# Retention and a squared-ReLU feed-forward on one core: the first four chunks stay in two-token rows through the attention

## The chip, the cores and the metric

The kernel runs on one core of a Trainium2 chip. The metric is device time in microseconds (us), as the median of several runs. One further execution is profiled; every row, wait and chain quoted in this document comes from such a profiled execution, and "the span" is its length from the first to the last recorded event.

The core has five engines with a queue each. TensorE (PE) multiplies matrices and also transposes, VectorE (DVE) and ScalarE (ACT) do elementwise work and are the ones that read TensorE's output memory PSUM, GpSimd (POOL) does elementwise work on SBUF alone, and SyncE (SP) issues the transfers (DMA) here.

## The reference

Two stages. The first is a retention layer: per batch (4) and head (8) a 64x64 state runs over 768 tokens, decays by a factor gamma of its head at each token and takes in the outer product of k and v; the output is q times the state, scaled. The second is a feed-forward on the 3072x512 result.

```python
for t in range(S):
    state = gamma[None, :, None, None] * state + np.einsum('bhd,bhe->bhde', k[:, :, t], v[:, :, t])
    y[:, :, t] = scale * np.einsum('bhd,bhde->bhe', q[:, :, t], state)
...
h = np.maximum(x @ w_in, 0.0)
return (h * h @ w_out).astype(np.float32)
```

Here x is y laid out as tokens by 512 features, w_in is 512x2048 and w_out is 2048x512. Inputs and output are float32; the kernel computes in bf16 with float32 accumulation.

## The kernel before

**Tiles.** The 3072 tokens are 24 chunks of 128 (six per batch). The recurrence is done in blocks: inside a state step the contribution of tokens is q times k, masked, times v; what came earlier is q times the state. Decay is put into tables, so that v is multiplied by `vf` (a growing factor per token) when it is cast, and the result by `yf` (a falling one) when it leaves PSUM. A state step covers 64 tokens, so a chunk has two. Per chunk the attention issues, on TensorE, `scores` (line 576, q times k into the PSUM tile `sc`), `sums` (line 587, k times v for the state, also into `sc`), `values` (line 550, masked scores times v into `yy`) and `apply` (line 565, q times state into `yy`). A `visit` is one such round; DVE then masks the scores (`P`, line 630), updates the state twice (`S`, lines 641 and 643), and multiplies the output into the feed-forward's input tile `xt` (`Y`, line 652). All matmuls of a visit are 64x64x64, spread over the four quadrants of the array.

**The first four chunks** come in two pairs (`together`, two calls, chunks 0 and 1, then 2 and 3). A pair's q, k and v are loaded so that a partition holds two neighbouring tokens (512 bytes in a piece in place of 256), one 512 KB transfer for each of q, k, v. They are cast into `twin` tiles (which live in the third hidden tile `h2`, shown as `h` in the profile). Then q and k are transposed on TensorE (`T`, line 434) and copied out (`E`), and k and v are put into normal token order by matmuls with a 0/1 matrix `perm` (`N`, line 459), each with a copy out of PSUM (`M`). After that the ordinary visits follow. Later chunks are loaded one by one; their q and k are transposed on TensorE (line 533) for chunks 4 to 7 and by a DMA after that.

**Feed-forward.** `ffn1` multiplies `xt` with `w_in` (line 699) block by block; a block is 1, 2 or 4 chunks (`BLOCKS`), and a group of matmuls always fills one PSUM bank (16 matmuls of 128 columns, 8 of 256 or 4 of 512). ACT applies ReLU (line 704), DVE squares (line 709). `ffn2` multiplies with `w_out` (line 743), four matmuls of 512 columns per quarter of w_out, ACT copies out (line 751) and SP stores.

**Weights** are loaded as float32 in pieces (`w_in` as four half quarters of 512 KB and two quarters of 1 MB, `w_out` as four quarters of 1 MB) through four staging tiles `wst` and cast in parts by DVE, ACT or POOL.

**Order.** Nothing is ordered by hand except the transfers, whose order is the string `ORDER` (`q0` is the q load of the first pair, `i0` the first piece of w_in, `o0` of w_out). Everything else is added to a `Plan` with an engine or several to choose from, assumed durations, the tiles it reads and writes, and a priority; `schedule` places the operations one after another, the earliest start first, and the program is emitted in that order, so that each engine's queue is fixed in advance. The plan also inserts filler matmuls on the identity (line 794), and `PRE` = 20 matmuls of one element at the very start (line 790). `SPLIT` says how many visits are split into two halves, `NPE` and `NTD` where the transposes change their kind (chunks from NPE to NTD are transposed by small flips inside a visit).

Of the kernel before, what the change touches and what calls it, by code (L numbers as in the profile page):

```python
# [15 lines left out]
ALU = mybir.AluOpType  # L16


class Plan:
# [21 lines left out]
    def add(self, name, eng, dur, reads=(), writes=(), fn=None, prio=0.0, lat=0.0, bank=None, after=(), count=0):  # L41
# [15 lines left out]
        if not isinstance(eng, dict):  # L57
            eng, flex = {eng: dur}, False
        else:
            flex = True  # L60
        self.ops.append(dict(i=i, name=name, eng=eng, flex=flex, deps=sorted(deps), fn=fn,
# [136 lines left out]
BLOCKS = [2, 1, 1, 1, 1, 2, 2, 2, 4, 4, 4]  # L198
SPLIT = 6
AHEAD = 4  # L200
WARM = 16.0
FILL = 0.215
WARMING = 5.5
PACE = 6
LEAD = 2
NPE = 8
NTD = 8
PRE = 20
# [3 lines left out]
TCAST = {'ACT': 0.63, 'POOL': 0.78}  # L212
TEVAC = {'ACT': 0.6}
MEVAC = {'ACT': 0.6, 'DVE': 0.62}
# [8 lines left out]

ORDER = (
    "o0 k0 v0 o1 q0 v2 k2 o2 q2 o3 i0 i1 i2 i3 q4 i4 v4 i5 k4 k5 v5 q5 k6 v6 q6 q7 v7 k7"
# [11 lines left out]
def kernel(  # L237
# [38 lines left out]
    def sb(name, shape, dt):  # L276
# [16 lines left out]
    perm = sb("perm", [P, 2, P], BF16)  # L293
    ex2_i = sb("ex2_i", [P, NCH // 2, 2], I32)
    ex2_f = sb("ex2_f", [P, NCH // 2, 2, H], FP32)
    vf2 = sb("vf2", [P, NCH // 2, 2, H], FP32)
# [5 lines left out]
             for j in range(2)]  # L302
    pos_i = h2s[NH2 - 1][:, 12:15, :].rearrange("p a n -> p (a n)").bitcast(I32)
# [15 lines left out]
    def where(m):  # L319

        return divmod(m, NCH)
# [27 lines left out]
    def placing():  # L349

        nc.gpsimd.memset(perm[:], 0.0)
        for half in range(2):
            r = slice(L * half, L * half + L)
            nc.gpsimd.affine_select(out=perm[r], in_=perm[r], compare_op=ALU.not_equal,
                                    fill=1.0, base=0, pattern=[[-1, 2], [1, P]], channel_multiplier=-2)
# [7 lines left out]
    pl.add("perm", "POOL", 1.2, (), ("perm",), placing, prio=-95.5)  # L363
# [15 lines left out]
               out=ex2_f[:], in0=ex2_i[:, :, :, None].to_broadcast([P, NCH // 2, 2, H]),  # L379
               in1=lng[:, None, None, :].to_broadcast([P, NCH // 2, 2, H]), op=ALU.mult), prio=-99)  # L380
# [5 lines left out]
    def ytable():  # L386
        for p in range(NJ):
            nc.scalar.activation(yf[:, p, :], pos_i[:], AF.Exp, scale=lnt[:, p : p + 1])
    yf_made = pl.add("yf", "ACT", 3.4, ("pos_i", "lnt"), ("yf",), ytable, prio=-98)
# [10 lines left out]
    twin_users = [yf_made]  # L400

    def together(n):
# [3 lines left out]
        m, s0, w, twin = 2 * n, (2 * n) % NLD, n % 2, twins[n % 2]  # L406
# [8 lines left out]
        for g in range(2):  # L415
            for x in "kq":
                o = twin[x][:, g, :].rearrange("s (j a d) -> s a j d", a=2, j=NJ)
                t = rows_(x).rearrange("s (a j g d) -> s a j g d", a=2, j=NJ, g=2)[:, :, :, g, :]
                pl.add(f"c{x}{m}.{g}", TCAST, 0, held(x), (f"twin{x}{w}.{g}",),
                       lambda on, t=t, o=o: copy_on(on, o, t), prio=urgency(m))  # L420
            t = rows_("v").rearrange("s (h g d) -> s h g d", h=H, g=2)[:, :, g, :]
            pl.add(f"cv{m}.{g}", CVT, 0, held("v") + ("vf2",), (f"twinv{w}.{g}",),
                   lambda on, t=t, g=g: (nc.vector if on == "DVE" else nc.gpsimd).tensor_tensor(  # L423
                       out=twin["v"][:, g, :].rearrange("s (h d) -> s h d", h=H), in0=t,
                       in1=vf2[:, i // 2, g, :, None].to_broadcast([P, H, D]), op=ALU.mult),
                   prio=urgency(m))
        q0 = m % NQT
        for x, name in enumerate("kq"):
            o1 = {}

            def turn_fn(g, x=x, name=name, o1=o1):
                ps = fps[o1["op"]["bank_index"]].bitcast(BF16)
                for j in range(NJ):
                    nc.tensor.transpose(ps[:, 512 * g + j * P : 512 * g + j * P + P],  # L434
                                        twin[name][:, g, j * P : j * P + P], ident[:])
            for g in range(2):
                i0 = pl.add(f"T{name}{m}.{g}", "PE", 0.26, (f"twin{name}{w}.{g}", "ident"), (f"gT{name}{m}{g}",),
                            lambda g=g, turn_fn=turn_fn: turn_fn(g),
                            prio=-200 + m, lat=0.2, count=4, after=twin_users[-1:] if g else (),
                            bank=("open", ("T", m, x), False) if g == 0 else ("use", ("T", m, x)))  # L440
                twin_users.append(i0)
                if g == 0:
                    o1["op"] = pl.ops[i0]
            for c in range(2):
                pl.add(f"E{name}{m}.{c}", TEVAC, 0,
                       [f"gT{name}{m}{g}" for g in range(2)], [f"qkT{q0 + c}.{name}"],
                       lambda on, x=x, c=c, o1=o1: copy_on(
                           on, qkts[q0 + c][:, x].rearrange("p j (t g) -> p j t g", g=2),
                           fps[o1["op"]["bank_index"]].bitcast(BF16).rearrange("p (g j c t) -> p c j t g", g=2, j=NJ, c=2)[:, c]),
                       prio=urgency(m + c), lat=0.05, bank=("close", ("T", m, x), 2))  # L450
        for c in range(2):
            r = slice(L * c, L * c + L)
            for name in "kv":
                o1 = {}

                def place(name=name, r=r, o1=o1):
                    ps = fps[o1["op"]["bank_index"]]
                    for g in range(2):
                        nc.tensor.matmul(ps[:], lhsT=perm[r, g, :], rhs=twin[name][r, g, :], start=(g == 0), stop=(g == 1))  # L459
                i0 = pl.add(f"N{name}{m + c}", "PE", 0.45, (f"twin{name}{w}.0", f"twin{name}{w}.1", "perm"), (f"gN{name}{m + c}",),  # L460
                            place, prio=-190 + m + c, lat=0.2, count=2, bank=("open", ("N", m + c, name), False))
                twin_users.append(i0)
                o1["op"] = pl.ops[i0]
                o = bf[name][(m + c) % NBF]
                o = o.rearrange("s j a d -> s (j a d)") if name == "k" else o.rearrange("s h d -> s (h d)")
                pl.add(f"M{name}{m + c}", MEVAC, 0, (f"gN{name}{m + c}",), (f"bf{name}{(m + c) % NBF}",),
                       lambda on, o=o, o1=o1: copy_on(on, o, fps[o1["op"]["bank_index"]][:]),
                       prio=urgency(m + c), lat=0.05, bank=("close", ("N", m + c, name)))
# [122 lines left out]
    def visit(m, n, t=None):  # L591
# [55 lines left out]
        if m is not None:  # L647
# [3 lines left out]
            pl.add(f"Y{m}", "DVE", 0.68, ("yy0", "yy1", "yf"), (f"xt{g % NXT}.{u}",),  # L651
# [29 lines left out]
    def ffn1(blk):  # L681
# [5 lines left out]
        for f0 in range(0, NFB, per):  # L687
# [19 lines left out]
            def square(f0=f0):  # L707
# [10 lines left out]
                   after=twin_users if g == NH2 - 1 else ())  # L718
# [45 lines left out]
    for m in range(-1, NM):  # L764
# [5 lines left out]
        if n < SPLIT:  # L770
            if m >= 0:
                visit(m, None)
            visit(None, n, t)
        else:
            visit(m, n if n < NM else None, t)
# [52 lines left out]
```

## Time and profile before

| | us |
|---|---|
| median of 6 runs | 212.51 (212.14 to 212.95) |
| the profiled execution | 212.11 |
| its span | 210.3 |
| TensorE busy in the span | 198.4 (94%) |
| VectorE busy | 115.5 (55%) |
| ScalarE busy | 90.9 (43%) |
| GpSimd busy | 42.8 (20%) |
| first feed-forward matmul starts | 19.79 |
| last matmul ends | 207.11 |

TensorE's busy time is the union of matmuls whose ends are modelled, so 94% is a share of time with something in the array, not of its peak. Where a row of the timeline ends in brackets, they give the idle time before it and what ended it. "Issue" in a chain is time in which the engine waited for nothing that the profile shows. In a list of waits the engine and line that waited come first, then what was waited for, the total, the number of times and the longest.

### The profile page before, as it was taken

How to read it: one execution, taken by the hardware profiler on the slowest of the kernel's cores; microseconds unless marked ns; L12 is line 12 of the kernel's file. 1: busy time of each engine (PE TensorE's matmuls, PEld its weight loads, DVE VectorE, ACT ScalarE, POOL GpSimd, SP SyncE). 2: the span in 40 equal slices, each digit the busy share in tenths (PEclk: the TensorE clock that was granted, in tenths of full speed). 3: DMA queues.
4: the chain of work that ended last, by engine and by line, in shares of the span. 5: the costliest groups of instructions: out<-in, count | busy, mean ns of one | idle time of the engine just before them, and what ended most of it. 6: DMA issues, size and time to landing. Idle time of an engine off the chain costs nothing.

```text
span 210.3 us, 6166 instructions
## 1 busy us (share of the span) xinstructions
PE 198.4 (94%) x2683; PEld 117.8 (56%) x2683; DVE 115.5 (55%) x253; ACT 90.9 (43%) x154; POOL 42.8 (20%) x72
## 2 busy tenths in 40 slices
PE   1797899999999999999999999999999999999993
PEld 1354798676766858767644444444444444444452
DVE  2557977866565956676756573667554433322100
ACT  8575667552332524444222644323533324534221
POOL 6653313233322211312222031222000000000000
PEclk9999999999999999999999999999999999999999
DMA  6999999999999999999999999999211011011022
GB/s 160 290 315 324 348 354 344 342 188 251 218 191 248 196 209 221 212 169 243 208 204 176 191 248 166 238 211 227 49 53 53 0 65 38 0 50 51 0 103 100
DMA packets 94443, 38.15 MB, mean 181 GB/s; under 512 B 79952, under 2 KB 88400, under 8 KB 94416
## 3 DMA queue, kind: packets, MB, share of 16 engines
q1 hardware_dynamic: 94416, 37.76, 83.4%
q8 instruction: 21, 0.34, 0.7%
q14 instruction: 6, 0.05, 0.1%
HBM read 27.26 MB, written 6.29 MB: 160 GB/s over the span
## 4 chain that ended last, share of the span: by engine, by line
PE 92%; DMA 3%; issue 1%; SPq 1%; POOL 1%; ACT 0%
PE fps L743 40%; PE fps L699 40%; DMA vn<-in_v_dram 3%; PE yy L550 3%; PE yy L565 2%; PE sc L587 2%; PE sc L576 2%; SPq L411 1%; PE fps L459 1%; PE fps L533 1%; POOL h L423 1%; PE fps L434 1%; PE fps L794 0%; ACT osb L751 0%
## 5 line engine op out<-in xcount | busy, mean ns | idle before, releaser
L743 PE MATMUL fps<-w_out,h 128*128 128x512 bf16 (+1 forms) x400 | 92.4, 371 | 0.0
L699 PE MATMUL fps<-xt,w_in 128*128 128x128 bf16 (+2 forms) x704 | 92.4, 282 | 0.0
L704 ACT ACTIVATE h<-fps 128x512 bf16<-128x512 f32 x96 | 57.3, 597 | 71.3 <-PE fps L699 71.2
L699 PEld LDWEIGHTS <-w_in 128*128 128x128 bf16 x704 | 58.3, 98 | 28.7
L709 DVE TENSOR_TENSOR h<-h 128x512 bf16<-128x512 bf16 x96 | 42.7, 452 | 52.5 <-ACT h L704 52.2
L743 PEld LDWEIGHTS <-h 128*128 128x128 bf16 x400 | 37.3, 98 | 36.9
L751 ACT ACTIVATE osb<-fps 128x512 f32<-128x512 f32 (+1 forms) x25 | 14.5, 580 | 35.8 <-PE fps L743 35.8
L397 POOL CAST kqs<-kn 128x512 bf16<-128x512 f32 x20 | 13.3, 666 | 66.1 <-DMA kn<-in_k_dram 58.2
L652 DVE TENSOR_TENSOR xt<-yy,yf 128x512 bf16<-128x512 f32 x24 | 16.5, 686 | 13.8 <-PE yy L565 12.6
L643 DVE TENSOR_TENSOR state<-sc,state 128x256 bf16<-128x256 f32 x40 | 16.8, 419 | 0.7
L630 DVE TENSOR_TENSOR pt<-sc,cmask 128x512 bf16<-128x512 f32 x24 | 16.4, 682 | 1.4 <-PE sc L587 1.2
L491 DVE TENSOR_TENSOR vs<-vn,vf 128x512 bf16<-128x512 f32 x20 | 15.1, 757 | 2.1 <-DMA vn<-in_v_dram 1.9
L397 POOL CAST kqs<-qn 128x512 bf16<-128x512 f32 x20 | 13.0, 650 | 11.9 <-DMA qn<-in_q_dram 11.8
L565 PE MATMUL yy<-qkT,state 64*64 64x64 bf16 x352 | 11.9, 198 | 0.5
L550 PEld LDWEIGHTS <-vs 64*64 64x64 bf16 x384 | 5.1, 107 | 8.5 <-issue 8.1
L587 PE MATMUL sc<-vs,kqs 64*64 64x64 bf16 x352 | 7.8, 195 | 1.5 <-issue 1.5
L393 ACT ACTIVATE qkT<-fps 128x512 bf16<-128x512 bf16 x12 | 6.7, 596 | 5.2 <-PE fps L533 3.1
L550 PE MATMUL yy<-pt,vs 64*64 64x64 bf16 x384 | 7.8, 198 | 0.6 <-issue 0.6
L434 PE MATMUL fps<-ident,h 128*128 128x128 bf16 x32 | 3.8, 273 | 4.5 <-POOL h L397 4.5
L565 PEld LDWEIGHTS <-state 64*64 64x64 bf16 x352 | 7.3, 107 | 1.1 <-PE yy L565 1.1
L576 PE MATMUL sc<-qkT 64*64 64x64 bf16 x384 | 7.6, 196 | 0.0
L587 PEld LDWEIGHTS <-kqs 64*64 64x64 bf16 x352 | 5.6, 109 | 1.6 <-issue 1.6
(51 smaller groups left out, 69.6 us busy)
## 6 DMA issues: line engine op xcount, KB each, us to landing
out_dram<-osb SPq DMA_DIRECT2D x23, 256.0 KB, 4.0
qn<-in_q_dram SPq DMA_DIRECT2D x20, 256.0 KB, 5.3
vn<-in_v_dram SPq DMA_DIRECT2D x20, 256.0 KB, 4.7
kn<-in_k_dram SPq DMA_DIRECT2D x20, 256.0 KB, 5.3
wst<-in_moe_w_out_dram SPq DMA_DIRECT2D x4, 1024.0 KB, 10.0
wst<-in_moe_w_in_dram SPq DMA_DIRECT2D x4, 512.0 KB, 8.4
wst<-in_moe_w_in_dram SPq DMA_DIRECT2D x2, 1024.0 KB, 10.1
kn<-in_k_dram SPq DMA_DIRECT2D x2, 512.0 KB, 5.8
```

What stands on the lines that cost most here:

```text
L397: nc.gpsimd.tensor_copy(o, t)
L491: lambda: nc.vector.tensor_tensor(out=o[:], in0=t.rearrange("s (h d) -> s h d", h=H), in1=vf[:, i, :, None].to_broadcast([P, H, D]), op=AL ...
L550: nc.tensor.matmul(yy[L * c : L * c + L, sub, p * L : p * L + L], lhsT=vs[r, 4 * a + j, :], rhs=pt[r, a, j, :], start=(p == 0), stop=True, ...
L565: nc.tensor.matmul(yy[L * c : L * c + L, sub, p * L : p * L + L], lhsT=st[r, j, :], rhs=qkT[r, 1, j, sub * L : sub * L + L], start=False, ...
L587: nc.tensor.matmul(sc[L * a : L * a + L, sub, 256 + j * D : 256 + j * D + D], lhsT=ks[r, j, a, :], rhs=vs[r, 4 * a + j, :], start=False, s ...
L630: lambda: nc.vector.tensor_tensor(out=pt[:], in0=sc[:, :, 0:256].rearrange("s g (p t) -> s g p t", p=NJ), in1=cmask[:, None, None, :].to_b ...
L643: f = lambda cc=cc, j1=j1, j0=j0: nc.vector.tensor_tensor(out=sts[j1][:], in0=cc, in1=sts[j0][:], op=ALU.add)
L652: lambda: nc.vector.tensor_tensor(out=xt[:, :, u * C : u * C + C].rearrange("s p (g t) -> s g p t", g=2), in0=yy[:, :, 0:256].rearrange("s ...
L699: nc.tensor.matmul(ps[:, u * n : u * n + n], lhsT=w_in_bf[j][:, cb, c * P : (c + 1) * P], rhs=xt[:, cb, cols], start=(cb == 0), stop=(cb = ...
L704: nc.scalar.activation(h2[:, f0 : f0 + per, cols], ps[:].rearrange("p (u n) -> p u n", u=per), AF.Relu)
L709: nc.vector.tensor_mul(hv, hv, hv)
L743: nc.tensor.matmul(ps[:, 0:w], lhsT=h2[:, fb, u * C : u * C + C], rhs=w_out_bf[j][:, c, ns], start=(fb == 0), stop=(fb == NFB - 1))
```

## The change

The pairs are no longer put into normal token order. The eight `N` products with `perm` (two matmuls each) and the eight copies `M` go, and with them `perm`. Instead the attention of the first four chunks works on a pair as it lies, with g the place of a token in its two-token row (0 or 1) and c the half of the partitions (so c is the chunk): scores and masked scores are made per g (`pair_scores`, `P`), the state step is 128 tokens (one per chunk), and `pair_values` and `pair_sums` add the two places in PSUM. The matmuls of `pair_scores`, `pair_values` and `pair_apply` have 128 columns. The work is divided by halves of the heads (b2): `sc` serves one half, `yy` the other. So a pair has two `A` (scores, 16 matmuls each), four `P`, two `B` (sums, 16 each; the last chunk of a batch would need none), two `S`, two `C` (values and state, 20 to 24 matmuls with a drain and a wait between the two parts of the state) and two `Y`.

What else changes with it: the casts of a pair are divided by heads (`.0`, `.1`) and may also run on DVE; a half's transposes have a bank of their own and one copy out, four per pair, on ACT or DVE; masked scores of a pair (`pts2`) live in the second hidden tile, so that its ReLU waits for the pairs; `yf` is made in four separate operations; chunks 2 and 3 form one block of the feed-forward; there are no one-element matmuls at the start (`PRE` 0); chunk 7 is transposed by flips (`NPE` 7); the order of the transfers changes; and a few casts are bound to an engine (`HOME`).

The core of the diff:

```diff
+        if name in HOME:
+            eng = {HOME[name]: eng[HOME[name]]}
+        prio = RANK.get(name, prio)
...
-BLOCKS = [2, 1, 1, 1, 1, 2, 2, 2, 4, 4, 4]
+BLOCKS = [2, 2, 1, 1, 2, 2, 2, 4, 4, 4]
-WARM = 16.0
+WARM = 20.0
-PACE = 6
+PACE = 8
-NPE = 8
+NPE = 7
-PRE = 20
+PRE = 0
-TCAST = {'ACT': 0.63, 'POOL': 0.78}
-TEVAC = {'ACT': 0.6}
-MEVAC = {'ACT': 0.6, 'DVE': 0.62}
+TCAST = {'DVE': 0.43, 'ACT': 0.63, 'POOL': 0.78}
+TEVAC = {'ACT': 0.6, 'DVE': 0.62}
...
+HOME = {'ck5': 'ACT', 'cq5': 'ACT', 'Eq0.0': 'DVE', 'cv0.0': 'DVE', 'ck0.0': 'DVE', 'cwin5.2': 'DVE', 'cv2.1': 'POOL', 'ck2.0': 'DVE', 'cwin5.0': 'DVE', 'cwin2.0': 'POOL', 'cwout0.3': 'POOL', 'cwin1.0': 'POOL', 'ck0.1': 'DVE', 'ck2.1': 'DVE'}
 ORDER = (
-    "o0 k0 v0 o1 q0 v2 k2 o2 q2 o3 i0 i1 i2 i3 q4 i4 v4 i5 k4 k5 v5 q5 k6 v6 q6 q7 v7 k7"
+    "q0 k0 o0 i0 v0 q2 k2 o1 v2 i1 v4 i2 k4 i3 i4 q4 i5 k5 v5 v6 o2 o3 q5 v7 k6 q6 k7 q7"
 )
...
-    perm = sb("perm", [P, 2, P], BF16)
+    cmask2 = sb("cmask2", [P, 2, C], BF16)
+    pts2 = [h2s[1][:, 4 * j : 4 * j + 4, :].rearrange("p (b a) (g j t) -> p b a g j t", b=2, g=2, j=2) for j in range(2)]
...
-                        nc.tensor.matmul(ps[:], lhsT=perm[r, g, :], rhs=twin[name][r, g, :], start=(g == 0), stop=(g == 1))
...
+    def pair_scores(m, b2):
+        t = pair_qk(m)
+        for g in range(2):
+            for j in range(2):
+                for a in range(2):
+                    r = slice(L * a, L * a + L)
+                    for c in range(2):
+                        nc.tensor.matmul(held_by[b2][L * c : L * c + L, a, (2 * g + j) * C : (2 * g + j + 1) * C],
+                                         lhsT=t[r, 0, b2, c, j, L * g : L * g + L], rhs=t[r, 1, b2, c, j, :],
+                                         start=(g == 0 and j == 0), stop=True, skip_group_check=True)
...
+    def pair_sums(m, c, ps):
+        kt, vt = pair_tiles(m)
+        r = slice(L * c, L * c + L)
+        for g in range(2):
+            for j in range(NJ):
+                for a in range(2):
+                    nc.tensor.matmul(ps[L * a : L * a + L, j * D : j * D + D], lhsT=kt[r, j, a, g, :], rhs=vt[r, 4 * a + j, g, :],
+                                     start=(g == 0 and j == 0), stop=True, skip_group_check=True)
...
+            for a in range(2):
+                pl.add(f"P{m}.{b2}{a}", "DVE", 0.68, (banks[b2][a], "cmask2"), (f"ptp{w}.{b2}{a}",),
...
+            def values_and_state(b2=b2):
+                pair_values(m, b2)
+                pair_apply(m, b2, 0)
+                nc.tensor.drain(fusable=True).then_inc(turn, 1)
+                turns[0] += 1
+                nc.tensor.wait_ge(turn, turns[0])
+                pair_apply(m, b2, 1)
...
-                   after=twin_users if g == NH2 - 1 else ())
+                   after=twin_users if g == NH2 - 1 else pt_users if g == 1 else ())
...
-        if n < SPLIT:
-            if m >= 0:
+        if n < 2 * NPAIR:
+            if n % 2 == 0:
+                pair_visits(n)
+        elif n < SPLIT or m < 2 * NPAIR:
+            if m >= 2 * NPAIR:
```

## The prediction

> **What bounds the kernel now.** I read the page's engine shares first, then TensorE's list of waits, then the chain of waits at the start and around 44 us, then the timeline for when tiles of the inputs arrive.
>
> ```profile
> PE 198.4 (94%) x2683; PEld 117.8 (56%) x2683; DVE 115.5 (55%) x253; ACT 90.9 (43%) x154; POOL 42.8 (20%) x72
> ```
>
> ```profile
> PE fps L434 <- POOL h L397: 4.5, 1, 4.5
> PE sc L587 <- issue: 1.5, 1, 1.5
> PE fps L459 <- DVE kqs L395: 0.8, 1, 0.8
> ...
> PE yy L550 <- issue: 0.6, 1, 0.6
> ```
>
> TensorE bounds it. Its few waits are all early, and the list holds only what its queue waited for; so the question is how early it becomes full, and how much work it then has. The chain, start, length and what:
>
> ```profile
> 12.18 1.04 PE fps L459 x4
> ...
> 15.33 0.54 PE fps L459 x2
> ...
> 17.28 0.53 PE fps L459 x2
> ...
> 18.16 1.48 issue
> 19.64 0.22 PE sc L587 x4
> 19.86 1.85 PE fps L699 x16
> ...
> 25.77 0.61 issue
> ```
>
> ```profile
> 42.88 1.79 PE fps L699 x32
> 44.67 0.86 PE fps L743 x4
> ...
> 195.83 11.28 PE fps L743 x68
> 207.13 0.38 ACT osb L751
> ```
>
> The reordering matmuls (L459) stand three times on the chain, 2.1 us in all, the feed-forward begins at 19.79, and after the stop at 25.77 there is no further one: TensorE works through to 207.11, and a tail of 3.2 us (copy, store) closes the span of 210.3. The two "issue" stops come after 449 and 705 TensorE instructions of the program (weight loads and matmuls counted), 256 apart. The times at which inputs are there are read where a cast starts that waited for a DMA:
>
> ```profile
> 5.21 1.17 POOL L397 CAST h<-kn 128x512 bf16<-128x512 f32 x2 [0.84 <-DMA kn<-in_k_dram]
> 7.03 1.54 POOL L423 TENSOR_TENSOR h<-vn,vf 128x512 bf16<-128x512 f32 x1 [0.66 <-DMA vn<-in_v_dram]
> ...
> 15.65 0.61 POOL L397 CAST w_in<-wst 128x512 bf16<-128x512 f32 x1 [0.88 <-DMA wst<-in_moe_w_in_dram]
> ```
>
> Likewise 8.73, 10.53, 12.33, 14.15 for the other pair loads: one 512 KB pair load per 1.8 us. Half pieces of w_in come at 15.65, 17.16, 19.71, 21.32 (1.5 us each, later ones shared with a q load), and the last quarter of w_out at about 42.6.
>
> **What the skill says.** "Runtime: NRT & Kernel Launch", Instruction fetch mechanics: instructions are refilled in blocks of 256, at a cost "mostly hidden". The 256 between the two stops fits; hidden they are not here, 1.48 and 0.61 us. The DMA view shows one instruction packet between 17.0 and 17.5 and one between 23.6 and 24.1: TensorE passed its 193rd instruction at 14.1 and resumed past the 449th at 19.64 (5.5 us later), passed that and resumed past the 705th at 26.38 (6.7 us later). So while inputs stream, a block needs 5.5 to 6.7 us from the passing of the edge before. "TensorE: Matmul & The Clock Gate", Part 1: the clock is halved until about 3.4 us of sustained work. The trace agrees: two 256-column fillers take 0.61 us at 13.15 and 0.38 at 16.25. Same page, Part 3: matmuls in different quadrants run concurrently; the trace shows 16 scores of 64 columns in 0.13 us on the chain, four at a time. "VectorE: DVE Perf Modes", mode 2x_2P: PSUM has one read port, so no doubled rate from there; masking 128x512 out of PSUM takes 0.682 us here, a cast from SBUF 0.41.
>
> **The change part by part.** Removed: 16 matmuls `N` (2.1 us on the chain, the rest before 10) and eight copies `M` of 0.6 to 0.69 us, four each on DVE and ACT. Added on DVE: four more `P` (0.682 each) and five casts (0.41 to 0.43). The 20 one-element matmuls at the start (0.64 us at 0.77, while nothing else could run) cost nothing either way, except that the 40 instructions less move the block edges. Two costs are not shown: a matmul of 64x64x128, and an interleaving copy of q out of PSUM on DVE. The first lies between 16 in 0.13 us (bound by issue, no dearer than 64 columns) and 16 in 0.45 (two at a time at 56 ns each); I take four at a time (16 matmuls of 128 columns take 0.89 us in the feed-forward, 56 ns each), 0.23, at half clock 0.43. The second lies between 0.425 (plain bf16 copy, DVE row) and 0.69 (cast from PSUM); I take 0.65. Below nothing neither can be.
>
> I walk the new queues with these rows. Loads: q0 5.2, k0 6.95, w_in piece 0 8.45, v0 10.25, q2 12.05, k2 13.85, v2 15.65, w_in piece 1 17.15. q casts and transposes 5.2 to 6.7, k casts on DVE to 7.85, copies of q and k to 8.65 and 9.2, scores at half clock until 9.9. Then v0: its POOL half takes 1.54 and ends at 11.8; `B` from 11.87 to 12.95; DVE meanwhile does v 10.96, two masks 12.32, `S` twice until 13.42, last mask 14.1. `C` of half 0 starts at 13.47 (0.95 at half clock), `Y` ends 15.2; `C` of half 1 ends 15.65 and its `Y` 16.4. The second pair's scores half 0 go at 16.65, and **the feed-forward starts at 17.0** in place of 19.79: weights and `xt` are there.
>
> From there DVE sets the pace, with nothing idle: copy of k 16.85, masks 17.8 and 18.5, third mask 19.2, `S` 19.7 and 20.15 (behind `B` at 18.85, which waits for both v casts of 1.54 on POOL), last mask 20.85, one square 21.3, the v cast of chunk 4 22.0, `Y` 22.7 and 23.4. TensorE does three groups of the first block (0.875 each) in between and then stands until 23.45 for `xt` of chunks 2 and 3. From there it is full: 13 groups of 256 columns (11.4), 4 of 128 (3.6), 6 quarters of ffn2 (5.2), three transposes (0.65), one visit in halves and a half (1.1) make 21.9 and reach the first product with the last quarter of w_out at **45.4**. That quarter: three small loads more stand ahead of it than before (786 KB, 2.25 us at 350 GB/s), so it lands at 44.9 and is cast at about 45.8. I take **45.8**.
>
> What remains then, against the kernel before at 44.67, where it starts the same product: two groups of 128 columns (1.79), one ffn2 quarter (0.865) and half a visit (0.2) less, and transposes: five of 0.22 before, two plus a round of flips (0.26) now, 0.4 less. So 207.11 - 44.67 - 3.25 = 159.2, TensorE ends at 205.0, the span is 208.2. Every hop between engines in the early walk was put at 0.05 us; I allow 0.4 for what is late there. **Span 208.6**, execution 210.4; the profiled execution of before is 0.4 below its median, so the median becomes **210.8**.
>
> The instruction stops: edge 193 is passed in the first `C` at 13.8, so the block past 449 (in the third `C`, 20.3) is there at 19.3 to 20.5, hidden by the wait for DVE; the next edge, 705, is not reached before 31. Cover gone, 0.2 us. Waits added: `C` waits on `S` and mask, and behind it stand transposes of the next pair and a feed-forward group; they are counted above. ReLU of the second hidden tile now waits for both pairs, long done by then. Casts of w_in on POOL stand behind three v casts: piece 1 at 19.4 and piece 2 at 20.2 instead of landing plus 0.6; that delays the second group to 19.4, under DVE's chain.
>
> **Rivals.** (1) The clock is late: TensorE's early work is sparser than before (idle from 9.9 to 11.87, hardly any fillers), so full clock may come only 3.4 us after 17.0. Then the first group takes 1.71, the scores of half 1 of the second pair end at 19.4 in place of 18.3, every DVE step after moves by 0.9 and TensorE is full at 24.35: the product with the last quarter starts at 46.3 plus the same 0.4, so 211.3. For it: 17.0 to 20.4 is the first unbroken stretch; against: before, some 5 us of nearly unbroken work (8.8 to 14) were enough to raise it. (2) The weights are late: loads share 16 engines, and one v load took 9 us from issue to landing in the trace before. With pieces 2 us later than worked out the last quarter is ready at 47.8; the equal point of the kernel before is 207.1 - 159.2 = 47.9: 212.4. (3) Slower, by one mechanism: half clock until 24. The first group, then scores and `B`, each doubled, put the second group at 20.6 to 22.35, then both `C` (1.1 each) until 24.3, then a group of 1.75, and only then the blocks of chunks 2 and 3: full at 26.2, with one more doubled group. The last-quarter product starts at 49.0 in place of 46.2: 213.6. It turns to slower when that product starts after 48.3; against it, the clock of before, up by 15. (4) The change does nothing, because the arrival of data alone sets the start: against it, TensorE before stood for instruction blocks and reordering with its data landed (q2 at 14.15, pieces of w_in at 15.65 and 17.16, first group 19.79); 212.5.
>
> **How the numbers follow.** As worked out, 0.54 (own range 209.9 to 211.4: no wait for w_out and no late hop give -0.8, hops twice as late and a missed cover +0.6). Rival 1, 0.18, 211.0 to 212.0. Rivals 2 and 4 together 0.12. Rival 3, 0.16, 212.8 to 214. A measurement here tells about 0.2% (0.4 us) from no change, so faster is below 212.1. Faster: the first two without a sliver, 0.71; same 0.12; slower 0.17. The range 209.9 to 213.0 leaves out most of rival 3 and the case that 128 columns cost no more than 64.
>
> **What would show it.** Right: no L459 rows; first feed-forward matmul at about 17; no "issue" stop over 0.3 us before 30; a TensorE wait of about 0.8 for `Y` ending near 23.5; after it an unbroken chain, first product with the last w_out quarter near 45.8. Wrong: group durations near 1.7 us for 8 matmuls after 20 (rival 3), TensorE waiting for casts of w_in or w_out (rival 2), or waits after 46, where I assume none because the queues are alike and before had none.

## The result, and the profile after

The change makes the kernel 0.7% slower: 214.37 us (median of 30 runs, 212.94 to 216.26) against 212.69 (65 runs) for the kernel before beside it, a ratio of 1.0074 (95% interval 1.0058 to 1.0091). The forecast was 210.8. The profiled execution took 214.93, with a span of 213.2.

Engine shares and the chain of waits on the page of the kernel after:

```profile
PE 198.3 (93%) x2570; PEld 117.6 (55%) x2570; DVE 116.0 (54%) x253; ACT 88.1 (41%) x148; POOL 41.2 (19%) x69
...
PE 60%; DMA 19%; SPq 17%; DVE 1%; POOL 1%; issue 1%; ACT 0%; POOLq 0%
```

The shares look as before. The chain does not. On the page of the kernel before it was:

```profile
PE 92%; DMA 3%; issue 1%; SPq 1%; POOL 1%; ACT 0%
```

There 92% of it was TensorE; now 36% is transfers and the queue that issues them. TensorE's list of waits (engine, line and what it waited for; total, times, longest):

```profile
PE fps L447 <- DVE h L401: 6.1, 2, 5.5
PE fps L494 <- DVE h L434: 1.4, 1, 1.4
PE fps L851 <- POOL w_out L403: 1.3, 1, 1.3
PE sc L684 <- DMA qkT<-kqs: 1.1, 2, 0.7
PE fps L494 <- POOL h L434: 0.6, 1, 0.6
```

No reordering matmuls and no "issue" stop are left. But there are two waits behind the start that the kernel before did not have: for the cast of a w_out quarter, and for q and k transposed by DMA. TensorE's timeline (start, length, what, count, and in brackets the idle time before it):

```profile
17.89 1.89 PE L807 MATMUL fps<-xt,w_in 128*128 128x256 bf16 x8
...
20.84 1.05 PE L807 MATMUL fps<-xt,w_in 128*128 128x256 bf16 x8
...
25.18 5.29 PE L807 MATMUL fps<-xt,w_in 128*128 128x256 bf16 x47 [0.33 <-DVE xt L573]
...
48.95 1.89 PE L851 MATMUL fps<-w_out,h 128*128 128x512 bf16 x8 [1.27 <-POOL w_out L403]
```

The feed-forward starts at 17.89, 1.9 us sooner than before (19.79), yet its first group takes 1.89 us where the second takes 1.05: the clock is still halved and rises only at about 20.5 (this is read from the durations; the page's row of the granted clock shows nothing of it). TensorE is full from 25.18, and the first product with the last w_out quarter starts at 48.95; the equal point of the kernel before, by the prediction's count of the work left, was 47.9. GpSimd's timeline shows the casts of the last two quarters, after:

```profile
42.92 0.87 POOL L403 CAST w_out<-wst 128x512 bf16<-128x512 f32 x1 [4.45 <-DMA wst<-in_moe_w_out_dram]
48.03 0.87 POOL L403 CAST w_out<-wst 128x512 bf16<-128x512 f32 x1 [4.24 <-DMA wst<-in_moe_w_out_dram]
```

And before:

```profile
39.83 0.87 POOL L397 CAST w_out<-wst 128x512 bf16<-128x512 f32 x1 [2.03 <-DMA wst<-in_moe_w_out_dram]
42.61 0.87 POOL L397 CAST w_out<-wst 128x512 bf16<-128x512 f32 x1 [1.92 <-DMA wst<-in_moe_w_out_dram]
```

The last one starts 5.1 us behind the one before it, where it was 2.8 us. Why is read in the transfers. The DMA view from 12 to 42 us, in 40 slices of 0.75 us (busy tenths of the 16 DMA engines; GB/s), first the kernel before, then after:

```profile
DMA  9999999999999999999999999999999999999999
GB/s 293 298 336 348 350 348 366 339 352 323 267 287 375 380 357 302 264 369 376 380 385 393 380 343 302 298 366 368 351 298 301 354 361 404 371 385 386 334 287 248
DMA packets 11549, 10.22 MB, mean 341 GB/s; under 512 B 5736, under 2 KB 8472, under 8 KB 11544
```

```profile
DMA  9999999999559999999999999999999999835999
GB/s 289 290 290 305 343 350 367 292 250 225 93 71 309 339 344 410 366 339 314 279 325 339 399 410 399 398 337 286 300 386 366 341 283 234 148 76 152 404 388 382
DMA packets 11932, 9.16 MB, mean 305 GB/s; under 512 B 6384, under 2 KB 9386, under 8 KB 11928
```

Both kernels move the same bytes in all, but after has two holes, at 19.5 to 21 and 37.5 to 39.75, where the DMA engines are busy only half of the time and, in the second hole, as little as a third. In these 30 us it moves 1.06 MB less, 3.1 us at 341 GB/s. SP's queue around the holes (issuing time is the second column; L588 loads one chunk in pieces of 256 bytes, L781 a weight piece):

```profile
12.76 0.97 SPq L588 DMA_DIRECT2D vn<-in_v_dram  x1
13.78 1.99 SPq L588 DMA_DIRECT2D kn<-in_k_dram  x1
15.81 4.67 SPq L781 DMA_DIRECT2D wst<-in_moe_w_in_dram  x2
20.53 0.51 SPq L588 DMA_DIRECT2D qn<-in_q_dram  x1
...
30.22 3.73 SPq L588 DMA_DIRECT2D vn<-in_v_dram  x2
34.11 3.47 SPq L781 DMA_DIRECT2D wst<-in_moe_w_out_dram  x1
37.62 0.51 SPq L588 DMA_DIRECT2D qn<-in_q_dram  x1
```

Ahead of each hole stand two chunk loads in a row (v and k of chunk 4; v of chunks 5 and 6), then two weight loads and one, in whose issuing SP stands for 4.7 and 3.5 us while the engines run dry. In the kernel before no two chunk loads stand in a row until the last weight load is issued (33.8 us). The order meant here and below is the trace's. The string `ORDER` only ranks the loads: `o0`, third in it, is issued as late as 21.2 us.

### The profile page after: what moved, and what is told of

The parts are those of the page before. It is cut to its first block, busy times and chain, and to the rows that moved or that the text cites. A ratio compares the mean times of both kernels' runs of the same rounds, so it can differ in the third digit from the quotient of the medians.

```text
span 213.2 us, 5941 instructions
## 1 busy us (share of the span) xinstructions
PE 198.3 (93%) x2570; PEld 117.6 (55%) x2570; DVE 116.0 (54%) x253; ACT 88.1 (41%) x148; POOL 41.2 (19%) x69
## 4 chain that ended last, share of the span: by engine, by line
PE 60%; DMA 19%; SPq 17%; DVE 1%; POOL 1%; issue 1%; ACT 0%; POOLq 0%
PE fps L851 30%; PE fps L807 25%; SPq L588 8%; DMA qn<-in_q_dram 6%; DMA wst<-in_moe_w_out_dram 5%; SPq L781 4%; SPq L418 4%; DMA kn<-in_k_dram 3%; DMA qkT<-kqs 3%; DMA vn<-in_v_dram 2%; PE yy L658 2%; PE yy L673 1%; PE sc L684 1%; PE sc L695 1%; SPq L863 1%
## 5 line engine op out<-in xcount | busy, mean ns | idle before, releaser
L807 PE MATMUL fps<-xt,w_in 128*128 128x256 bf16 (+2 forms) x640 | 93.6, 296 | 0.4 <-DVE xt L573 0.3
L851 PEld LDWEIGHTS <-h 128*128 128x128 bf16 x400 | 37.7, 98 | 38.0 <-issue 1.2
L760 DVE TENSOR_TENSOR xt<-yy,yf 128x512 bf16<-128x512 f32 x20 | 13.7, 686 | 16.5 <-PE yy L673 12.2
L751 DVE TENSOR_TENSOR state<-sc,state 128x256 bf16<-128x256 f32 x33 | 13.8, 418 | 0.5
L738 DVE TENSOR_TENSOR pt<-sc,cmask 128x512 bf16<-128x512 f32 x20 | 13.6, 680 | 0.1
L673 PE MATMUL yy<-qkT,state 64*64 64x64 bf16 x296 | 10.0, 197 | 0.2
L684 PE MATMUL sc<-qkT 64*64 64x64 bf16 x320 | 6.3, 194 | 1.1 <-DMA qkT<-kqs 1.1
L399 ACT ACTIVATE qkT<-fps 128x512 bf16<-128x512 bf16 x8 | 4.7, 596 | 5.8 <-PE fps L447 4.7
L447 PEld LDWEIGHTS <-h 128*128 128x128 bf16 x32 | 3.0, 135 | 7.0 <-DVE h L401 6.4
L403 POOL CAST w_out<-wst 128x512 bf16<-128x512 f32 x5 | 3.7, 753 | 14.3 <-DMA wst<-in_moe_w_out_dram 14.3
L401 DVE CAST w_out<-wst 128x512 bf16<-128x512 f32 x7 | 4.3, 646 | 3.9 <-DMA wst<-in_moe_w_out_dram 3.9
```

Of the source, the lines that this page charges most:

```text
L403: nc.gpsimd.tensor_copy(o, t)
L673: nc.tensor.matmul(yy[L * c : L * c + L, sub, p * L : p * L + L], lhsT=st[r, j, :], rhs=qkT[r, 1, j, sub * L : sub * L + L], start=False, ...
L738: lambda: nc.vector.tensor_tensor(out=pt[:], in0=sc[:, :, 0:256].rearrange("s g (p t) -> s g p t", p=NJ), in1=cmask[:, None, None, :].to_b ...
L751: f = lambda cc=cc, j1=j1, j0=j0: nc.vector.tensor_tensor(out=sts[j1][:], in0=cc, in1=sts[j0][:], op=ALU.add)
L760: lambda: nc.vector.tensor_tensor(out=xt[:, :, u * C : u * C + C].rearrange("s p (g t) -> s g p t", g=2), in0=yy[:, :, 0:256].rearrange("s ...
L807: nc.tensor.matmul(ps[:, u * n : u * n + n], lhsT=w_in_bf[j][:, cb, c * P : (c + 1) * P], rhs=xt[:, cb, cols], start=(cb == 0), stop=(cb = ...
```

## The experiments

Every ratio is to the kernel before, run beside it. All moves below are made in the planned sequence, with this helper, so that nothing else in the plan changes:

```python
def move(name, after):
    sequence.remove(place[name])
    sequence.insert(sequence.index(place[after]) + 1, place[name])
```

**The late weights and the late clock, alone and together, and the instruction stops of the kernel before.** Four kernels: v of chunk 6 moved behind the last w_out quarter; five matmuls of 512 columns on the identity ahead of the first sums; both; and the kernel before without its 20 one-element matmuls.

```diff
# the weights
+    move('ldv6', 'ldwout3')
+    move('cv6', 'R2.12')
# the clock
+                for _ in range({'B0': 5}.get(o["name"], 0)):
+                    nc.tensor.matmul(fps[NBANK - 1][:, 0 : 4 * P], lhsT=ident[:],
+                                     rhs=ident[:, None, :].to_broadcast([P, 4, P]), start=True, stop=True)
# the kernel before
-            for _ in range(PRE):
+            for _ in range(0):
```

> The kernel after, with one transfer moved: the v load of chunk 6 (and its cast) goes behind the last quarter of w_out. Theory 1 (small loads fill the transfer queue and hold back w_out, and TensorE waits for that): the last quarter lands 1 to 2.5 us earlier than 48.0, TensorE's wait of 1.27 us for its cast goes, the time falls by 1.0 to 1.6 us. Theory 2 (the half clock until 20.5 us is what costs): w_out's wait is only where the lateness shows, no change within 0.3 us. Theory 3 (the pair products themselves are dearer): no change either.

Measured 213.06 (ratio 1.003, 1.0008 to 1.0052), 1.3 us better than the change, as theory 1 had it; the other two said no change. The last quarter's cast in GpSimd's timeline, and the DMA view from 12 to 42 us:

```profile
46.20 0.87 POOL L403 CAST w_out<-wst 128x512 bf16<-128x512 f32 x1 [3.25 <-DMA wst<-in_moe_w_out_dram]
```

```profile
DMA  9999999999869999999999999999999999999999
...
DMA packets 12296, 9.78 MB, mean 326 GB/s; under 512 B 6382, under 2 KB 9464, under 8 KB 12292
```

The cast comes 1.8 us sooner, though only one load of 0.75 us (262 KB at 350 GB/s) was taken from ahead of it: the second hole is gone too. (This profiled execution, 215.01, lies far above the kernel's median, by waits behind 50 us; only its early part is used.)

> The kernel after, with five dummy matmuls of 512 columns on the identity put before the first sums of the first pair, where TensorE stands idle from 9.65 to 11.97 us. Theory 2: full clock is there by 14 to 16 in place of 20.5, the feed-forward starts 0.7 to 1.3 us earlier than 17.89, chunks 2 and 3 follow 1 to 2 us earlier than 25.18, and the end 1 to 2 us earlier. Theory 1: the start moves just as much, but TensorE then waits longer for the last quarter of w_out (48.9 as before), and the time is the same within 0.4 us.

Measured 214.58 (1.0103, 1.0071 to 1.0134): nothing won, although the clock was full from 12.7. TensorE's timeline:

```profile
16.22 1.05 PE L807 MATMUL fps<-xt,w_in 128*128 128x256 bf16 x8
...
26.14 4.23 PE L807 MATMUL fps<-xt,w_in 128*128 128x256 bf16 x19 [1.91 <-POOL w_in L403]
```

The start is 1.67 us sooner, and then TensorE waits 1.91 us for a w_in piece; behind that wait the clock falls back (19 matmuls in 4.23 us, twice the 0.11 us each of warm ones). The time is what theory 1 said, but the wait that takes the gain is for w_in, not for the last w_out quarter.

> Both edits. Theory 1 with theory 2 behind it (two limits, one hiding the other): 2.0 to 3.0 us less than the kernel after, which is more than the sum of the two edits alone and at or below the kernel before. If w_out alone decides, no more than the transfer edit alone; if the clock alone decides, no more than the dummies alone.

Measured 213.57 (1.0061, 1.0039 to 1.0084): 0.8 us below the change, where 2.0 to 3.0 were expected, and no better than with the load moved alone. TensorE waits 1.5 us for w_in, 0.8 for another w_out quarter and 1.5 for k of chunks 4 and 6. So something else limits the kernel too; I took it to be either the order of the transfers or their amount.

> The kernel before, with its 20 one-element matmuls at the start left out and all else in the same order. If the two stops of TensorE at 18.16 (1.48 us) and 25.77 (0.61 us) are the fetch of instruction blocks, the edges now lie 40 instructions later in the program and the first stop goes or shrinks below 0.5 us; the time falls by 0.5 to 1.5 us. If the stop comes from something in the work itself, it stays at the same matmul and the time is the same within 0.3 us.

Measured 213.57 (1.0031, 1.0009 to 1.0053). The first "issue" stop is gone and the feed-forward starts at 18.77, a microsecond sooner, but the second stop grew:

```profile
27.14 0.22 PE L565 MATMUL yy<-qkT,state 64*64 64x64 bf16 x4 [1.64 <-issue]
```

It stands exactly 40 instructions later in the program than the stop of 0.61 us did (40 are the weight loads and matmuls left out). So the stops are tied to the place in the program, as the prediction took them; but moving the edges did not make the kernel faster by the expected 0.5 to 1.5 us, it made it 0.3% slower.

**Order or amount of the transfers.** Theories are numbered anew from here. One kernel has both edits and v and k of chunk 4 behind one more w_in piece; two are planned anew with another order of transfers, without and with the clock edit; one has eight chunks transposed on TensorE again.

```diff
# with both edits
+    move('ldk4', 'ldwin3')
+    move('ldv4', 'ldk4')
+    move('ck4', 'cwin3.0')
+    move('cv4', 'Q0.2')
+    move('Tk4', 'F1.1.0')
+    move('Ek4', 'R1.0')
# planned anew
-    "q0 k0 o0 i0 v0 q2 k2 o1 v2 i1 v4 i2 k4 i3 i4 q4 i5 k5 v5 v6 o2 o3 q5 v7 k6 q6 k7 q7"
+    "q0 k0 i0 v0 q2 k2 v2 i1 i2 i3 k4 i4 v4 q4 i5 o0 k5 o1 o2 q5 v5 o3 k6 v6 q6 q7 v7 k7"
# planned anew
-NPE = 7
+NPE = 8
```

> The kernel with both edits, and chunk 4's loads of v and k moved behind the fourth quarter of w_in in SP's order, with their conversions, transposes and copy moved behind it too. Theory 1 (the order of the transfers decides): the fourth quarter is cast about 2 us sooner than with both edits (24.8 there), TensorE's wait of 1.5 us for it goes, and the time falls by 1.0 to 1.5 us, to 212.1 to 212.6. Theory 2 (the sum of the transfers decides: SP's queue is never empty until 50 us, so whatever TensorE wins early it waits for later, at a w_out quarter or at k of chunk 5 or 6): the time stays within 0.4 us of 213.6, and the 1.5 us stand at later waits.

Measured 214.3 (6 runs; 1.0075, 1.0046 to 1.0103), 0.7 worse than with both edits (the two intervals overlap).

> The changed kernel planned anew with all of w_in's quarters ahead of chunk 4's loads, and w_out's quarters each ahead of the loads of v of chunks 5, 6 and 7; no matmuls to warm the clock. Theory 1: the last w_out quarter lands 3 to 4 us sooner than in the changed kernel (48.0), its wait goes, and the time is 212.6 to 213.4. Theory 2: no better than the kernel with the one load moved, 213.1 or more, with waits for k, q or v of chunks 5 to 7 in place of it.

Measured 213.16 (1.0031, 1.0016 to 1.0047).

> The same plan with five 512-column matmuls ahead of the first sums, to warm the clock. Theory 1: feed-forward 1.5 us sooner, no wait for w_in's fourth quarter or for w_out, 1.0 to 1.7 us less than without these matmuls: 211.0 to 212.2, below the kernel before. Theory 2: within 0.4 us of the same plan without them, the 1.5 us lost again to a later transfer.

Measured 213.41 (1.0036, 1.002 to 1.0052): no gain from the clock.

> The changed kernel planned anew with eight chunks transposed on TensorE, as in the kernel before, in place of seven, so that the first transposes by DMA come one chunk later. Theory 1 (q and k turned by DMA come too late for chunks 7 and 8, 1.1 us): those waits go, eight transposes of some 0.6 us are added, and the time falls by 0.3 to 0.8 us, to 213.6 to 214.1. Theory 2 (these waits only take the place of others): 214.2 to 214.8.

Measured 214.74 (6 runs; 1.0106, 1.008 to 1.0131). The wait for transposes by DMA fell from 1.1 to 0.6 us and nothing was won.

Two of the four fell into theory 2's range, and the first lies 0.3 above it, outside both; the new order without the clock edit, 213.16, fits either theory. So I took the amount to be the cause; the next runs were to settle it.

**Fewer bytes.** The loads of chunks 4 to 7 bring half of the heads, in the kernel after, in the one with the clock edit, and in the kernel before. The output of these three is not the layer's; they tell times alone.

```diff
-                   lambda x=x, t=t: nc.sync.dma_start(
-                       t.rearrange("s (h d) -> s h d", h=H),
-                       src[x][b, :, i * C : (i + 1) * C, :].rearrange("h s d -> s h d")),
+                   lambda x=x, t=t, hs=slice(0, 4 if m < 8 else H): nc.sync.dma_start(
+                       t.rearrange("s (h d) -> s h d", h=H)[:, hs],
+                       src[x][b, hs, i * C : (i + 1) * C, :].rearrange("h s d -> s h d")),
```

> The changed kernel, whose loads of q, k and v of chunks 4 to 7 bring only four of the eight heads (the other four keep what the buffers held, so the output is not the reference's): 12 transfers halved, 1.57 MB fewer, some 4.5 us of transfers at the 350 GB/s of this stretch, about half of it ahead of the last w_out quarter; every other instruction is as before. Theory 2 (the sum of the transfers bounds both kernels up to about 50 us): the last w_out quarter is cast about 2 us sooner (48.0), the waits for w_out and for q and k turned by DMA (1.3 and 1.1) shrink, 212.2 to 213.4. Rival (TensorE's own work and the order of it bound the kernel, and the waits only take each other's place): 213.9 or more.

Measured 211.02 (0.9933, 0.9911 to 0.9956), 3.4 us below the change, more than the 1 to 2.2 that theory 2 expected. The chain of waits on its page is TensorE's again:

```profile
PE 89%; DMA 3%; DVE 2%; issue 1%; SPq 1%; ACT 1%; POOL 1%; ACTq 0%; DVEq 0%; POOLq 0%
```

> The same with the five matmuls that warm the clock. Theory 2: without the shortage of transfers the 1.7 us won by the clock come through to the end: 1.2 to 1.9 us below the one without these matmuls, 210.6 to 211.8, about what was predicted for the change. Rival: no gain from the clock here either, within 0.4 us of the one without.

Measured 209.41 (6 runs; 0.9854, 0.9808 to 0.99), 1.6 below the one without the five matmuls, as theory 2 had it, on a level that is lower throughout. Now the clock's gain is there in full.

> The kernel before with the same loads halved. Theory 2: it has no wait for transfers to lose, and is faster by at most 0.5 us: 212.1 to 212.7. Rival (transfers bound the kernel before just as much): 1 us faster or more, 211.6 or less.

Measured 212.59 (0.9999, 0.9974 to 1.0024): fewer bytes are worth nothing to the kernel before. So transfers take the change's gain, and they did not bound the kernel before. But the halved loads of the kernel after also have no hole left in the DMA view, and from 12 to 42 us they moved 10.08 MB, more than the 9.16 of the full ones. So halving took away bytes and holes at once, and these three runs cannot tell which of the two the shortage came from. That led back to SP's queue, and to theory 3, that two chunk loads in a row make the holes.

**The same bytes without pairs of chunk loads, and the kernel before with one.** To the move of v of chunk 6, k of chunk 4 is moved behind one w_in piece, without and with the clock edit; in the kernel before k of chunk 5 is put directly behind k of chunk 4.

```diff
# on top of the moves of v of chunk 6
+    move('ldk4', 'ldwin3')
+    move('ck4', 'cwin3.0')
+    move('Tk4', 'F1.1.0')
+    move('Ek4', 'R1.0')
# the kernel before
+    move('ldk5', 'ldk4')
```

> The changed kernel with the load of v of chunk 6 moved behind the last w_out quarter, as in the first experiment, and the load of k of chunk 4 moved behind one w_in piece (its conversion, transposes and copy follow it), so that ahead of every weight load stands at most one load of 256-byte pieces; no byte fewer. Theory 3 (two such loads in a row ahead of a weight load leave half of the DMA engines without work while SP stands in issuing): no slice below 280 GB/s between 16 and 42 us, where the changed kernel has two such holes, at 18 to 22 and 36 to 40; 0.5 to 1 us faster than with v of chunk 6 moved alone (213.06): 212.0 to 212.6. Theory 2 (the sum of the bytes bounds): 212.9 to 213.9, as the other orders.

Measured 212.61 (14 runs; 1.0002, 0.9977 to 1.0027): 1.8 us better than the change, level with the kernel before, and at the upper edge of theory 3's range (212.6), below theory 2's. Its DMA view and the last quarter's cast:

```profile
DMA  9999999999999899999999999999999999999999
GB/s 287 292 289 298 343 344 362 312 271 275 342 283 193 251 394 388 357 317 301 380 356 388 388 390 390 317 278 317 388 360 332 300 301 344 375 342 295 268 367 364
DMA packets 12339, 9.86 MB, mean 329 GB/s; under 512 B 6400, under 2 KB 9471, under 8 KB 12335
```

```profile
45.44 0.87 POOL L403 CAST w_out<-wst 128x512 bf16<-128x512 f32 x1 [3.28 <-DMA wst<-in_moe_w_out_dram]
```

Of the first hole a shallow one of 193 is left, and five more slices lie at 251 to 278, against the expectation of none below 280; TensorE waits for no w_out quarter any more.

> The same with the five matmuls that warm the clock. Theory 3: with the holes gone the clock's gain comes through, at least in part: 0.8 to 1.7 us below the same order without these matmuls, 210.8 to 211.8, and faster than the kernel before. Theory 2: no gain from the clock, 212.9 to 213.9.

Measured 212.74 (22 runs; 1.0002, 0.9984 to 1.002). This part of theory 3 failed: the clock's gain did not come through, as theory 2 had said. TensorE's waits of this kernel:

```profile
PE fps L641 <- POOL kqs L403: 1.1, 2, 0.6
PE fps L807 <- DVE xt L573: 0.8, 2, 0.5
PE sc L684 <- DMA qkT<-kqs: 0.5, 1, 0.5
PE fps L851 <- issue: 0.5, 3, 0.2
PE sc L504 <- issue: 0.4, 1, 0.4
```

It now waits for k of chunks 4 and 6. Loading k and q of chunk 6 ahead of v of chunks 6 and 7 would tell whether the last of these limits it; no run shows that.

> The kernel before, with one load moved: k of chunk 5 goes ahead of the second w_out quarter, directly behind k of chunk 4, so that two loads of 256-byte pieces stand in a row ahead of weight loads; no byte more. Theory 3: a hole below 250 GB/s in the transfers some 5 us later, at about 30 to 34 us, where the kernel before has 319 or more; the w_out quarters land 1 to 1.5 us later, and as the kernel before has 2 us to spare for the last of them the time rises by 0 to 0.8 us. Theory 2: no hole, and within 0.2 us of the kernel before.

Measured 213.67 (14 runs; 1.0054, 1.0033 to 1.0075), 1.0 us slower for one load moved. SP's queue, first in the kernel before, then here:

```profile
22.69 2.15 SPq L480 DMA_DIRECT2D kn<-in_k_dram  x1
25.01 1.36 SPq L673 DMA_DIRECT2D wst<-in_moe_w_out_dram  x1
26.42 3.40 SPq L480 DMA_DIRECT2D kn<-in_k_dram  x1
```

```profile
22.90 3.69 SPq L480 DMA_DIRECT2D kn<-in_k_dram  x2
26.70 6.39 SPq L673 DMA_DIRECT2D wst<-in_moe_w_out_dram  x3
```

The DMA view here:

```profile
DMA  9999999999999999999999999954789998999999
GB/s 290 303 341 350 348 346 359 344 360 311 262 299 384 381 359 271 298 378 374 377 388 385 383 341 259 248 96 117 83 180 385 396 358 262 407 401 391 404 396 381
DMA packets 10130, 9.75 MB, mean 325 GB/s; under 512 B 4425, under 2 KB 7110, under 8 KB 10125
```

A hole stands at 31.5 to 34.5 us where the kernel before had 298 to 368 GB/s, and the last w_out quarter is cast at 44.25 in place of 42.61. The time is 0.2 more than the upper end of the expectation. In this one execution the chain of waits has 74% for TensorE, not 92. Its clock is also halved from about 19.75 to 23.5 us, ahead of the hole, but that is not the difference: runs of the kernel before have it too (last section), and at a like granted clock the moved load costs 1.7 us (213.4 against 211.7, clock 0.997 or more) and 1.2 us (213.9 against 212.7, clock 0.990 to 0.992).

All kernels that load every byte; the pairs are two chunk loads in a row with a weight load behind them, holes are slices below 180 GB/s in the DMA view from 12 to 42 us:

| kernel | pairs | holes near | MB, 12 to 42 us | us |
|---|---|---|---|---|
| before | none | none | 10.22 | 212.69 |
| before, no one-element matmuls | none | none | 10.21 | 213.57 |
| before, k of chunk 5 moved | k4 k5 | 33 | 9.75 | 213.67 |
| after | v4 k4; v5 v6 | 20, 38 | 9.16 | 214.37 |
| clock | v4 k4; v5 v6 | 20, 39 | 9.05 | 214.58 |
| NPE 8 | v4 k4; v5 v6 | 20, 38 | 9.43 | 214.74 |
| v6 moved | v4 k4 | 20 | 9.78 | 213.06 |
| both | v4 k4 | 20 | 9.52 | 213.57 |
| both, k4 and v4 moved | k4 v4 | 21 | 9.69 | 214.3 |
| new order | v4 q4 | 26 | 9.54 | 213.16 |
| new order, clock | v4 q4 | 26 | 9.47 | 213.41 |
| v6 and k4 moved | none | none | 9.86 | 212.61 |
| the same with the clock | none | none | 9.92 | 212.74 |

Up to 42 us every pair has its hole and no hole is without its pair. (The bound of 180 was drawn afterwards; the lowest slices without a pair are 192 and 193.) That the pair causes the hole is shown in both directions, with one profile of each kernel: taken apart in the kernel after, put together in the kernel before.

Two things limit this. First, holes come behind the last weight load too, where chunk loads stand in a row in every kernel: at about 42.5 us in the kernel before (84 to 120 GB/s in slices of 0.3 us), and at about 45 us in the one with v6 and k4 moved (86 to 158), where v of chunks 6 and 7 now stand together. So a weight load behind the pair is not needed for a hole; what a good order does is to let the hole fall behind the last w_out quarter. Second, the amount of bytes still counts. The kernel after with halved loads is 1.6 us below the one with v6 and k4 moved (211.02 against 212.61), though both are without holes up to 42 us; and the clock edit wins 1.6 us with halved loads and nothing with full ones.

Why the DMA engines run dry is not shown. In the second hole of the kernel after, from 37.5 to 39 us, 592 of 602 packets are smaller than 512 bytes: the end of the pair is still moving, and the pieces of the next weight load are not there yet. A long issue alone makes no hole: with v6 and k4 moved SP stands 3.52 us in a w_out load at 26.59, and none follows. The Trainium skill, "DMA: Bandwidth & Descriptors", Specifications, says that transfers reach the full rate only from 512 bytes on; a chunk load has pieces of 256. That agrees with these loads being the slow kind, but single ones lower the rate only to 264 to 302 GB/s in the kernel before, and two halved ones in a row, with as many bytes as one whole, made no hole (no slice below 265 up to 36 us); so the piece size alone does not explain it.

## Why the prediction was wrong

**Held.** The reordering matmuls went and nothing took their place on the chain; 16 products of 128 columns cost 0.25 us warm and 0.44 cold from start to start (0.23 and 0.43 taken); the first `C` started at 13.28 and the second ended at 16.0 (13.47 and 15.65 by the walk); no "issue" stop is left. With fewer bytes to move and a warm clock the change is worth 3.2 us (209.41 against 212.59). From 25.18 until TensorE stood for the last quarter, at 47.68, it was 22.5 us of work; 21.9 were worked out.

**The step that failed first: "that quarter ... lands at 44.9 and is cast at about 45.8".** Its cast began at 48.03 and was done at 48.90, 3.1 us late. The step counted three loads more ahead of it, 2.25 us at 350 GB/s, as if the rate did not depend on the order. By 42 us the kernel after was 3.1 us of transfers behind the kernel before, with two holes. With the pairs broken up, and one chunk load less ahead of the quarter, the cast began at 45.44, and the time fell by 1.76 us (214.37 to 212.61). This step alone set the product's start: TensorE was ready for it at 47.68.

**The clock.** The walk took half clock for the products up to `C` and full clock for the feed-forward's first group; it was rival 1, with 0.18, that let it rise at 20.4. It rose at about 20.5, and TensorE was full at 25.18 where the walk had 23.45 and rival 1 24.35. I had argued from the kernel before, whose clock was up by 15 after "nearly unbroken work". Part of that work were the reordering matmuls of 512 columns that the change removes; the products that stay, transposes and 64-row products, left the clock down for 8 us of nearly unbroken work (11.97 to 20.5), more than twice the 3.4 us that the prediction took from Part 1. Five matmuls of 512 columns brought it up by 12.7 (by about 14 in two other kernels with them); they also fill a stretch in which TensorE stood idle, so whether the kind of work or the gap matters more is not separated. For transposes the Trainium skill, "TensorE: Matmul & The Clock Gate", Part 4, says that in transpose mode the full clock does not engage, since it does not count as busy in the same way. I had used Part 1 of that page and not Part 4. No run here has transposes alone; once the clock is up they do run at the full rate, four in 0.40 us in place of 0.61. The term is worth 1.6 us (211.02 to 209.41), but only where transfers are not short.

**"Waits after 46, where I assume none because the queues are alike".** There were 1.27 us for w_out at 48.95 and 1.1 for q and k turned by DMA, at 70 and 83. The queues were alike in length, not in how far behind they were: the first transpose by DMA was issued at 58.97 us in place of 57.47.

**The chances.** Late weights and a late clock were two rivals, and each alone ended below the kernel before (212.4 and 211.3). Both came, and with the waits behind them they end above it. The slower rival, half clock until 24, named the wrong mechanism; its product with the last quarter starts at 49.0, and the measured one at 48.95 only because of the weights. The two rivals do not exclude each other, and a case for both together was missing.

**The sum.** In the profiled execution the span is 213.2 where 208.6 was forecast. Of these 4.6 us, 2.75 are the last quarter's product (48.95 in place of 46.2, the walk's 45.8 with the 0.4 allowed for hops), 1.1 are the two waits behind it, and 0.7 lie in the rest of the work, worked out at 159.2; these I have not traced. By the medians 3.6 us are missing. The order of the loads is worth 1.8 of them. The other half stays with the transfers: no kernel here that loads every byte got it back, with or without the clock edit, and the kernel with halved loads and that edit (209.41) got more than all of it.

## What to carry to other kernels

When a change reorders loads, price the order, not only the bytes: look at SP's queue for two small-piece loads in a row ahead of a load that TensorE will wait for, and at the DMA view for slices in which the engines are not busy. When a change removes TensorE work, ask whether that work was what raised the clock. And when two rivals in a forecast can both be true, give the case of both its own chance and its own time.

## What the runs showed of the hardware that I had not expected

- Two loads of 1024 pieces of 256 bytes in a row left up to two thirds of the DMA engines' time idle for 1.5 to 3 us, some 6 to 9 us after the first of the two was issued. One such pair put into the kernel before cost 0.47 MB by 42 us, and 1.0 us in the end.
- The clock can fall after less than 2 us without work. TensorE's timeline of the kernel before with halved loads, behind its stop of 1.58 us:

```profile
19.89 0.22 PE L587 MATMUL sc<-vs,kqs 64*64 64x64 bf16 x4 [1.58 <-issue]
20.05 2.88 PE L699 MATMUL fps<-xt,w_in 128*128 128x256 bf16 x16
```

Sixteen matmuls take 2.88 us, and the granted clock is 0.5 from 20.75 to 24.25 us; behind the stop of 1.48 us in the kernel before they took 1.92. The clock also fell behind 1.66 us in the kernel before with k of chunk 5 moved and behind 1.91 us in the kernel with the clock edit, and did not behind 1.52 us in the one with both edits. It differs from run to run. Of 181 runs of the kernel before beside the experiments, 104 have a mean granted clock of 0.990 to 0.992 and a median of 212.7 us, 64 have 0.997 or more and 211.7, and 13 have 0.984 and 213.9. So a fall costs about 1 us, and most runs of the kernel before have one. Both profiles of it or its variants that show a fall have it right behind an "issue" stop; the kernel after has no such stop, and all its 30 runs have 0.997 or more. The change wins this, which the prediction did not count; against runs of the kernel before without a fall it loses 2.7 us, not 1.7.
- Removing one "issue" stop can enlarge the next: without the one-element matmuls, 1.48 and 0.61 us became none and 1.64.
